# A reordered opening in a one-core retention-and-GELU kernel: identity and single loads first, wider filler matmuls, w_in triggered behind A of batch 0, chunk 1 loaded in one queue

## The chip, the cores and the metric

The kernel runs on one core of a Trainium2 chip. The core has five engines that run their own instruction streams in order: TensorE (PE, with its weight loads shown apart as PEld), VectorE (DVE), ScalarE (ACT), GpSimd (POOL) and SyncE (SP). SP, ACT and POOL also issue DMAs, each into a queue of its own. The metric is the device time of one execution in microseconds (us).

## The reference

A retention recurrence for 4 batches, 8 heads, 768 positions and head size 64, followed by a two-matrix feed-forward block with a tanh GELU:

```python
gamma = 1.0 - 2.0 ** (-5.0 - np.arange(H))
for t in range(S):
    state = gamma[None, :, None, None] * state + np.einsum('bhd,bhe->bhde', k[:, :, t], v[:, :, t])
    y[:, :, t] = scale * np.einsum('bhd,bhde->bhe', q[:, :, t], state)
x = y.transpose(0, 2, 1, 3).reshape(B * S, H * D)          # 3072 x 512
h = x @ w_in                                               # 512 x 2048
g = 0.5 * h * (1.0 + np.tanh(c * (h + 0.044715 * h * h * h)))
out = g @ w_out                                            # 2048 x 512
```

All inputs and the output are float32.

## The kernel before

**Tiling.** The 768 positions are cut into six chunks of 128. For a chunk `c` and a batch `b` the attention part consists of small steps, each a group of PE instructions followed by a copy out of PSUM:

- `prep1`: q and k are scaled by decay columns of the constants `cst` and become f16, v becomes f16. The engine is an argument (VE, AC, PO stand for DVE, ACT, POOL).
- T (`mm_T`, `ev_T`): eight 128x128 transposes of q and k with the identity `iden`, and a copy to `qkT`.
- A (`mm_A`, `ev_A`): eight matmuls give the score tiles `a_ps`; DVE multiplies them by a mask into `a_sb`.
- Y (`mm_yc`, `mm_yi`, `ev_Y`): the part from the state (none in chunk 0) and eight matmuls of v with `a_sb`; the result becomes `xT`.
- S (`mm_s`, `ev_S`): the update of the state `st`.

The feed-forward part then works on `xT` of all four batches (512 columns): `moe1` computes h for one block of 128 of the 2048 features and applies GELU on ACT; `moe1_two` does two blocks for a part of the columns; `moe2` multiplies with `w_out`. Chunks 2 to 5 use a variant with fewer matmuls and more sums on DVE and POOL (`m1_parts`, `m2_parts`); the change does not touch it.

**Order.** The schedule is written by hand: each engine executes its instructions in the order of the program text. In the opening (lines 108 to 117) the loads of chunk 0 go out on SP and ACT. `load1` loads one batch (256 KB), `load2` two batches (512 KB), `load` a whole chunk (1 MB). The weights `w_in` and `w_out` are cast to f16 by DMAs that POOL issues (`load_w_in`, `load_w_out`, four of each); they stand in POOL's queue between its `prep1` steps.

`spin(n)` (line 126) issues `n` f32 matmuls of a zero tile into a PSUM bank whose content nobody reads; they are filler work for PE. In `before` the zero tile is f16 with 512 columns, read as f32 with 256 columns.

**Chunk 0** (lines 667 to 730): T, A and Y of the four batches with fillers between them, then h of features 0 to 3 in three column stages (batches 0 and 1, batch 2, batch 3), S, and `moe1` for features 4 to 15.

**Chunk 1's loads** (lines 732 to 763): q and k of chunk 1 use the same buffers as those of chunk 0. `hold` (line 106) lets POOL write one element of the q buffer after a given tile is there, so that SP's first load must wait for it: once for the third quarter of `w_out`, once for the GELU of feature 10. SP then loads q and k batch by batch. v of chunk 1 is loaded by ACT: batches 0 and 1 in the middle of `moe1` of chunk 0, 2 and 3 behind it. Then `run` interleaves `moe2` of chunk 0 (16 units) with attention steps of chunk 1 after given units. The loads of chunk 2's q and k follow behind all of that on SP.

PSUM has eight banks: two for tag "h", two for "o", four for "att", taken in turn.

Of the kernel before, what the change touches and what calls it, by code (L numbers as in the profile page):

```python
# [9 lines left out]
F16 = mybir.dt.float16  # L10
F32 = mybir.dt.float32
# [5 lines left out]
def kernel(  # L17
# [9 lines left out]
    nc = tc.nc  # L27
    B, H, S, Dh = q.shape
    C = 128
    NCk = S // C  # L30
    NHP = H // 2
# [19 lines left out]
    iden_h = nc.inline_tensor(iden_np, name="rr_ident")  # L51
# [5 lines left out]
    const = ctx.enter_context(tc.tile_pool(name="const", bufs=1))  # L57
    ld = ctx.enter_context(tc.tile_pool(name="ld", bufs=2 * B))
    pre = ctx.enter_context(tc.tile_pool(name="pre", bufs=2 * B))
    att = ctx.enter_context(tc.tile_pool(name="att", bufs=4))  # L60
# [27 lines left out]
    def load1(eng, nm, c, b):  # L88
        eng.dma_start(
            out=ld_tile(nm, c, b),  # L90
            in_=srcs[nm][b, :, c * C:(c + 1) * C, :].rearrange("h p d -> p h d"),
        )

    def load2(eng, nm, c, b):
        eng.dma_start(
            out=raw_of(nm, c)[:, b * H:(b + 2) * H],
            in_=srcs[nm][b:b + 2, :, c * C:(c + 1) * C, :].rearrange("b h p d -> p (b h) d"),
        )

    def load(nm, c, eng=nc.sync):  # L100
        eng.dma_start(
            out=raw_of(nm, c),
            in_=srcs[nm][:, :, c * C:(c + 1) * C, :].rearrange("b h p d -> p (b h) d"),
        )
# [3 lines left out]
        nc.gpsimd.tensor_copy(out=ld_tile(nm, c, b)[0:1, 0, 0:1], in_=until)  # L108

    nc.sync.dma_start(out=cst[:, :OT + 128], in_=cst_h.ap())  # L110
    load2(nc.scalar, "q", 0, 0)
    load2(nc.sync, "k", 0, 0)
    load2(nc.scalar, "q", 0, 2)
    nc.sync.dma_start(out=iden, in_=iden_h.ap())
    load2(nc.sync, "k", 0, 2)
    load2(nc.sync, "v", 0, 0)
    load2(nc.sync, "v", 0, 2)


    zero = const.tile([128, 512], F16, name="zero")  # L120
    nc.vector.memset(zero, 0.0)
    nc.scalar.activation(
        out=misc[:, 0:1], in_=zero[:, 0:1], func=AF.Gelu_apprx_tanh, scale=1.0
# [2 lines left out]
    def spin(n):  # L126
        ps = bank("h", shape=(128, 512), name="spin_ps")
        for _ in range(n):
            nc.tensor.matmul(  # L129
                out=ps[:, 0:256], lhsT=zero.bitcast(F32)[:, 0:128], rhs=zero.bitcast(F32), start=True, stop=True  # L130
            )


# [22 lines left out]
    def prep1(eng, nm, c, b):  # L156
        t = pre.tile(
            [128, H, Dh], F16, tag=f"{nm}16", bufs=B, name=f"{nm}16"
        )
        src = ld_tile(nm, c, b)  # L160
        if (nm == "v") == (c < 2):
            copy_on(eng, t, src)
        else:
            col = OQ if nm == "q" else OK
            eng.tensor_tensor(  # L165
                out=t,
                in0=src,
                in1=cst[:, col:col + H].unsqueeze(2).broadcast_to([128, H, Dh]),
                op=ALU.mult,
            )  # L170
        h16[nm, c, b] = t
# [5 lines left out]
    a_sb = {}  # L177
# [9 lines left out]
    def bank(tag, dt=F32, shape=(128, NHP, 128), name="ps"):  # L187
        turn[tag] += 1
        return bank_at(BANKS[tag][(turn[tag] - 1) % len(BANKS[tag])], dt, shape, name)
# [15 lines left out]
    def ev_T(c, b, eng=nc.vector):  # L205
        copy_on(eng, qkT_of(c, b), pss.pop(("T", c, b)))
# [8 lines left out]
    def mm_A(c, b):  # L215
        t = qkT[c, b]
        ps = [bank("att", name=f"a_ps{j}") for j in range(2)]
        for hp in range(NHP):
            for j in range(2):
                nc.tensor.matmul(  # L220
                    out=ps[j][:, hp],
                    lhsT=t[j * 64:(j + 1) * 64, 1, hp],
                    rhs=t[j * 64:(j + 1) * 64, 0, hp],
                    start=True,
                    stop=True,
                )
        pss["A", c, b] = ps

    def ev_A(c, b):
        ps = pss.pop(("A", c, b))  # L230
        for j in range(2):
            s = att.tile([128, NHP, 128], F16, tag=f"a{j}", bufs=2, name=f"a_sb{j}")
            nc.vector.tensor_tensor(out=s, in0=ps[j], in1=mask[:, j], op=ALU.mult)  # L233
            a_sb[c, b, j] = s

    def mm_yc(c, b, tag):
        y_ps = pss["Y", c, b] = bank(tag, name="y_ps")
        if c == 0:
            return

        for hp in range(NHP):
            for j in range(2):
                sl = slice(j * 64, (j + 1) * 64)
                nc.tensor.matmul(  # L244
                    out=y_ps[sl, hp],
                    lhsT=st[sl, b, hp],
                    rhs=qkT[c, b][sl, 0, hp],
                    start=(hp == 0),
                    stop=False,
                    skip_group_check=True,  # L250
                )

    def mm_yi(c, b):
        y_ps = pss["Y", c, b]
        for hp in range(NHP):
            for j in range(2):
                nc.tensor.matmul(  # L257
                    out=y_ps[j * 64:(j + 1) * 64, hp],
                    lhsT=h16["v", c, b][:, 2 * hp + j],
                    rhs=a_sb[c, b, j][:, hp],  # L260
                    start=(c == 0),
                    stop=True,
                    skip_group_check=True,
                )
# [78 lines left out]
    NO = 4  # L343
    w_out_sb = [const.tile([128, NF // NO, d_model], F16, name=f"w_out{i}") for i in range(NO)]

    def load_w_in(i):
        nc.gpsimd.dma_start(
            out=w_in_sb[i],
            in_=moe_w_in.rearrange("(kc p) n -> p kc n", p=128)[
                :, :, w_in_at[i] * 128:(w_in_at[i] + w_in_n[i]) * 128  # L350
            ],
        )

    def load_w_out(i):
        n = NF // NO
        nc.gpsimd.dma_start(
            out=w_out_sb[i],
            in_=moe_w_out.rearrange("(fc p) n -> p fc n", p=128)[:, i * n:(i + 1) * n],
        )
# [26 lines left out]
        moe1_mm(c, fc, h_ps, 0, B * C)  # L386
        gelu(g_tile(c, fc)[:, fc % 2], h_ps)

    def moe1_two(c, fp, t0, t1):

        h_ps = bank("h", shape=(128, 2, B * C // 2), name="h_ps")
        for r in range(2):
            moe1_mm(c, 2 * fp + r, h_ps[:, r, 0:t1 - t0], t0, t1)
        gelu(g_tile(c, 2 * fp)[:, :, t0:t1], h_ps[:, :, 0:t1 - t0])
# [269 lines left out]
    half = 2 * C  # L664


    def pre_T(b, after=0):
        spin(after)
        mm_T(0, b)
        ev_T(0, b, AC)  # L670

    spin(6)
    for b in (0, 1):
        prep1(VE, "q", 0, b)
        prep1(PO, "k", 0, b)
    load_w_in(0)
    pre_T(0)
    pre_T(1)
    spin(1)
    mm_A(0, 0)  # L680
    ev_A(0, 0)
    mm_A(0, 1)
    prep1(VE, "q", 0, 2)
    ev_A(0, 1)
    prep1(VE, "q", 0, 3)
    for b in (2, 3):
        prep1(PO, "k", 0, b)
    for i in range(1, 4):
        load_w_in(i)
    load_w_out(0)  # L690
    spin(2)
    pre_T(2)
    prep1(AC, "v", 0, 0)
    prep1(AC, "v", 0, 1)
    spin(2)
    mm_A(0, 2)
    ev_A(0, 2)
    mm_yc(0, 0, "o")
    mm_yi(0, 0)
    pre_T(3)  # L700
    mm_yc(0, 1, "o")
    mm_yi(0, 1)
    ev_Y(0, 0, AC)
    ev_Y(0, 1, VE)
    prep1(PO, "v", 0, 2)
    prep1(PO, "v", 0, 3)
    for i in range(1, NO):
        load_w_out(i)
    spin(1)
    mm_A(0, 3)  # L710
    ev_A(0, 3)


    t01 = (0, half)
    moe1_two(0, 0, *t01)
    mm_yc(0, 2, "o")
    mm_yi(0, 2)
    ev_Y(0, 2, AC)
    moe1_two(0, 1, *t01)
    mm_yc(0, 3, "o")  # L720
    mm_yi(0, 3)
    ev_Y(0, 3)
    for t in ((half, half + C), (half + C, 2 * half)):
        for fp in range(2):
            moe1_two(0, fp, *t)
    for bs in ((0, 1), (2, 3)):
        mm_s(0, bs)
        ev_S(0, bs)
# [4 lines left out]
    for fc in range(6, NF):  # L733
        moe1(0, fc)
        if fc % 2 and fc < 14:
            win_sums(VE, (fc - 7) // 2)
        if fc in (8, 10):
            load1(AC, "v", 1, (fc - 8) // 2)
        if fc == 11:
            hold("q", 1, 0, g_tile(0, 10)[0:1, 0, 0:1])  # L740

# [7 lines left out]
    def preps(c, b):  # L749
# [1 line left out]
        prep1(PO, "k", c, b)  # L751
        prep1(AC, "v", c, b)

    load1(SY, "q", 1, 0)
    load1(SY, "k", 1, 0)
    load1(SY, "q", 1, 1)
    load1(SY, "k", 1, 1)
    load1(SY, "q", 1, 2)
    load1(SY, "k", 1, 2)
    load1(SY, "q", 1, 3)  # L760
    load1(SY, "k", 1, 3)
    load1(AC, "v", 1, 2)
    load1(AC, "v", 1, 3)
    u = [units2(0, b, tag="ooho"[b]) for b in range(B)]
    run(
        [u[i % 3][i // 3] for i in range(12)] + u[3],
# [5 lines left out]
            8: [(preps, 1, 0)],  # L772
            10: [(att_T, 1, 0), (preps, 1, 1)],
            11: [(att_AY, 1, (), "att", 1, (0,), None)],
            12: [(att_T, 1, 1), (preps, 1, 2)],
            13: [(att_AY, 1, (0,), "h", 1, (1,), AC)],
            14: [(att_T, 1, 2), (preps, 1, 3), (att_S, 1, 0)],
            15: [(att_AY, 1, (1,), "h", 1, (2,), AC), (att_T, 1, 3), (att_S, 1, 1)],
# [2 lines left out]


    nc.sync.dma_start(out=dec.rearrange("p h t -> p (h t)"), in_=dec_h.ap())
    load("q", 2)
    load("k", 2)

    def cast(nm, c, *bs):
        for b in bs:
# [155 lines left out]
```

## Time and profile before

| What | Value |
|---|---|
| median of 3 runs | 206.59 us (206.44 to 206.8) |
| profiled execution | 206.57 us, span 204.8 us, mean granted PE clock 0.983 |
| DVE, ACT, POOL busy | 129.3, 119.4, 110.4 us |
| constants `cst`: issue, landing | 0.74 us, 2.3 us later |
| identity: issue to landing | 7.0 us |
| w_in, issue to landing (4 DMAs of 512 KB) | 6.7 to 11.4 us, median 8.5 |
| first w_in trigger, first w_out trigger | 8.76 us, 14.73 us |
| first q load of chunk 1 | 33.97 us |
| DMA: moved in the span | 33.73 MB, mean 165 GB/s |

The profiled execution has a span from the first to the last instruction and some 1.8 us around it. The page gives busy time of each engine, the chain of work that ended last (followed back from the last instruction to what released each step), and groups of instructions. The timeline lists instructions in order with start and duration, and what ended the idle time before. The granted clock is the share of full speed that PE's throttle allowed. Line numbers (L129 and the like) are those of the kernel before.

### The profile page before, as it was taken

Reading aid. Unit: us, or ns where it says so; the run is one execution under the profiler, and the core shown is the slowest. Engines: PE = TensorE matmul, PEld = TensorE weight load, DVE = VectorE, ACT = ScalarE, POOL = GpSimd, SP = SyncE. Lnnn points to the kernel's source line nnn. Section 1 sums busy time; section 2 is a strip of 40 time slices with the busy share of each in tenths; the row PEclk is TensorE's granted clock in tenths of the full one; section 3 lists DMA queues with packets and bytes.
Section 4 is the critical chain, followed back from the end, with each engine's and each line's share of the span. In section 5 each row is a group of like instructions: output and inputs, shape, how many; then the busy total and the mean of one; then the engine's idle time right before and its main releaser. Section 6 shows DMA issues by size and latency. Waiting matters only on the chain.

```text
span 204.8 us, 5174 instructions
## 1 busy us (share of the span) xinstructions
PE 194.8 (95%) x2104; PEld 154.1 (75%) x2104; DVE 129.3 (63%) x260; ACT 119.4 (58%) x225; POOL 110.4 (54%) x113
## 2 busy tenths in 40 slices
PE   7398999999999989999999999999999999999993
PEld 6375744445678877788887888888888888888882
DVE  2267399429876789889853888836697723445421
ACT  2036566133478458853978585878555687675411
POOL 0596000124104992826399948399955797599000
PEclk9769999999999999999999999999999999999999
DMA  7999999999899994479959979433100230002204
GB/s 160 284 233 223 207 206 214 287 216 277 256 326 230 275 283 78 103 98 299 274 126 215 255 199 244 103 130 131 26 3 0 90 118 0 5 0 102 106 25 179
DMA packets 60663, 33.73 MB, mean 165 GB/s; under 512 B 40864, under 2 KB 57632, under 8 KB 60640
## 3 DMA queue, kind: packets, MB, share of 16 engines
q1 hardware_dynamic: 44640, 23.18, 45.6%
q0 software_dynamic: 4304, 4.46, 12.7%
q10 hardware_dynamic: 11696, 5.77, 10.7%
q8 instruction: 16, 0.26, 0.5%
q14 instruction: 7, 0.06, 0.1%
HBM read 27.63 MB, written 6.29 MB: 166 GB/s over the span
## 4 chain that ended last, share of the span: by engine, by line
PE 86%; DMA 5%; DVE 3%; ACT 3%; issue 1%; SPq 0%; DVEq 0%
PE o_ps L510 28%; PE h_ps L625 23%; PE h_ps L366 14%; PE o_ps L400 7%; DMA iden<-rr_ident 3%; PE y_ps L257 3%; PE a_ps L220 3%; PE y_ps L244 3%; PE qkT_ps L195 3%; PE spin_ps L129 1%; PE s_ps L281 1%; DVE xT L273 1%; DMA qkT<-k 1%; ACT qkT L152 1%; ACT g L382 1%
## 5 line engine op out<-in xcount | busy, mean ns | idle before, releaser
L437 POOL TENSOR_TENSOR s_g<-g 128x512 f16<-128x512 f16 x34 | 38.7, 1152 | 11.8 <-ACT g L382 11.8
L382 ACT ACTIVATE g<-h_ps 128x512 f16<-128x512 f32 (+1 forms) x50 | 29.0, 581 | 19.9 <-PE h_ps L366 14.2
L233 DVE TENSOR_TENSOR a_sb<-a_ps,mask 128x512 f16<-128x512 f32 x48 | 30.2, 684 | 9.5 <-PE a_ps L220 7.9
L510 PE MATMUL o_ps<-t_w,s_g 128*128 128x256 f16 x240 | 34.2, 273 | 0.0
L510 PEld LDWEIGHTS <-s_g 128*128 128x128 f16 x320 | 31.3, 98 | 3.6
L366 PE MATMUL h_ps<-xT,w_in 128*128 128x256 f16 (+2 forms) x224 | 30.4, 288 | 0.1
L625 PE MATMUL h_ps<-t_x,s_w 128*128 128x256 f16 x192 | 28.9, 273 | 0.3 <-DVE h_p L437 0.3
L625 PEld LDWEIGHTS <-s_w 128*128 128x128 f16 x256 | 24.5, 98 | 4.5 <-issue 1.2
L366 PEld LDWEIGHTS <-w_in 128*128 128x128 f16 x224 | 19.7, 98 | 7.9 <-issue 0.2
L510 PEld LDWEIGHTS <-g 128*128 128x128 f16 x240 | 23.4, 98 | 2.8
L510 PE MATMUL o_ps<-w_out,g 128*128 128x256 f16 x160 | 22.9, 273 | 0.0
L437 POOL TENSOR_TENSOR s_g<-s_g,g 128x512 f16<-128x512 f16 x17 | 19.6, 1156 | 4.6 <-PE o_ps L510 3.4
L165 POOL TENSOR_TENSOR v<-v,cst 128x512 f16<-128x512 f32 x16 | 16.2, 1037 | 10.7 <-DMA v<-in_v_dram 10.7
L642 ACT COPY h_u<-h_ps 128x512 f32<-128x512 f32 x16 | 9.4, 586 | 21.3 <-PE h_ps L625 21.2
L437 DVE TENSOR_TENSOR h_q<-h_ps,h_q 128x512 f32<-128x512 f32 x16 | 11.1, 692 | 16.3 <-PE h_ps L625 10.5
L625 PEld LDWEIGHTS <-w_in 128*128 128x128 f16 x192 | 18.3, 98 | 3.4 <-issue 0.7
L437 DVE TENSOR_TENSOR h_p<-h_ps,h_p 128x512 f32<-128x512 f32 x16 | 11.0, 690 | 13.9 <-ACT h_p L642 9.6
L437 POOL TENSOR_TENSOR s_g<-g,s_g 128x512 f16<-128x512 f16 x17 | 19.5, 1155 | 0.5
L625 PE MATMUL h_ps<-xT,w_in 128*128 128x256 f16 x128 | 19.2, 272 | 0.3 <-ACT g L382 0.3
L165 POOL TENSOR_TENSOR k<-k,cst 128x512 f16<-128x512 f32 x8 | 8.4, 1054 | 18.1 <-DMA k<-in_k_dram 15.5
L437 DVE TENSOR_TENSOR o_sb<-o_ps,o_sb 128x512 f32<-128x512 f32 (+1 forms) x18 | 10.8, 597 | 7.6 <-PE o_ps L510 7.3
L400 PE MATMUL o_ps<-w_out,g 128*128 128x512 f16 x64 | 14.8, 379 | 0.0
(70 smaller groups left out, 302.4 us busy)
## 6 DMA issues: line engine op xcount, KB each, us to landing
out_dram<-o_sb SPq DMA_DIRECT2D x8, 512.0 KB, 2.7
w_in<-in_moe_w_in_dram POOLq DMA_DIRECT2D x4, 512.0 KB, 8.5
w_out<-in_moe_w_out_dram POOLq DMA_DIRECT2D x4, 512.0 KB, 13.7
q<-in_q_dram ACTq DMA_DIRECT2D x2, 512.0 KB, 6.0
k<-in_k_dram SPq DMA_DIRECT2D x2, 512.0 KB, 5.6
v<-in_v_dram SPq DMA_DIRECT2D x2, 512.0 KB, 8.0
v<-in_v_dram ACTq DMA_DIRECT2D x4, 256.0 KB, 6.5
q<-in_q_dram SPq DMA_DIRECT2D x4, 256.0 KB, 5.2
```

Source lines behind the costliest of these rows:

```text
L165: eng.tensor_tensor(out=t, in0=src, in1=cst[:, col:col + H].unsqueeze(2).broadcast_to([128, H, Dh]), op=ALU.mult,)
L195: nc.tensor.transpose(out=ps[:, i, hp], in_=pair(h16[nm, c, b], hp), identity=iden)
L220: nc.tensor.matmul(out=ps[j][:, hp], lhsT=t[j * 64:(j + 1) * 64, 1, hp], rhs=t[j * 64:(j + 1) * 64, 0, hp], start=True, stop=True,)
L233: nc.vector.tensor_tensor(out=s, in0=ps[j], in1=mask[:, j], op=ALU.mult)
L244: nc.tensor.matmul(out=y_ps[sl, hp], lhsT=st[sl, b, hp], rhs=qkT[c, b][sl, 0, hp], start=(hp == 0), stop=False, skip_group_check=True,)
L366: nc.tensor.matmul(out=out, lhsT=w_in_sb[wi][:, kc, wr * 128:(wr + 1) * 128], rhs=xT[c][:, kc, t0:t1], start=(kc == 0), stop=(kc == NHP - ...
L382: nc.scalar.activation(out=out, in_=in_, func=AF.Gelu_apprx_tanh, scale=1.0)
L400: nc.tensor.matmul(out=ps[:, n0:n1], lhsT=g_sb[c, fc // 8][:, fc % 8, b * C:(b + 1) * C], rhs=w_out_sb[fc // (NF // NO)][:, fc % (NF // NO ...
L437: eng.tensor_tensor(out=out, in0=in0, in1=in1, op=op)
L510: nc.tensor.matmul(out=po, lhsT=lhs(c, lk, fp, a), rhs=rhs(rk, fp), start=(new and fp == 0 and (last or a == 0)), stop=(fp == NP - 1), ski ...
L625: nc.tensor.matmul(out=p[:, f], lhsT=w, rhs=x, start=(new and f == 0 and kk == 0), stop=(kk == 1), skip_group_check=True,)
L642: nc.scalar.copy(out=snap[nm], in_=p)
```

## The change

The change touches the opening and the loads of chunks 1 and 2.

- Loads: q and k of batches 0 and 1 are loaded singly, alternating between ACT and SP; the identity goes out on ACT second, not on SP third; k of batches 2 and 3 on SP and q of batches 2 and 3 on ACT follow.
- The zero tile becomes f32 with 512 columns, and a filler matmul takes all 512.
- `a_sb` gets four buffers for each half, where it had two.
- The opening's order: T(0), A(0), T(1), A(1), T(2), T(3), A(2), Y(0), A(3), Y(1), Y(2), then h, with fillers of 8, 2, 2, 3, 1 and 1. q of batch 2 is scaled ahead of A(1)'s masks. A one-element copy on POOL that reads `a_sb` of batch 0 stands ahead of the first `load_w_in`, and with it behind A(0). The last `w_in` and all of `w_out` follow behind the casts of v for batches 2 and 3.
- h of batch 2's columns uses the "att" banks.
- Chunk 1: q, k and v all go on SP, v in pairs of batches behind k of batches 1 and 2; the whole q of chunk 2 follows on SP at once, and k of chunk 2 is issued behind unit 12.

```diff
     nc.sync.dma_start(out=cst[:, :OT + 128], in_=cst_h.ap())
-    load2(nc.scalar, "q", 0, 0)
-    load2(nc.sync, "k", 0, 0)
+    load1(nc.scalar, "q", 0, 0)
+    load1(nc.sync, "k", 0, 0)
+    nc.scalar.dma_start(out=iden, in_=iden_h.ap())
+    load1(nc.sync, "q", 0, 1)
+    load1(nc.scalar, "k", 0, 1)
+    load2(nc.sync, "k", 0, 2)
     load2(nc.scalar, "q", 0, 2)
-    nc.sync.dma_start(out=iden, in_=iden_h.ap())
-    load2(nc.sync, "k", 0, 2)
     load2(nc.sync, "v", 0, 0)
     load2(nc.sync, "v", 0, 2)
...
-    zero = const.tile([128, 512], F16, name="zero")
+    zero = const.tile([128, 512], F32, name="zero")
...
             nc.tensor.matmul(
-                out=ps[:, 0:256], lhsT=zero.bitcast(F32)[:, 0:128], rhs=zero.bitcast(F32), start=True, stop=True
+                out=ps, lhsT=zero[:, 0:128], rhs=zero, start=True, stop=True
             )
...
-            s = att.tile([128, NHP, 128], F16, tag=f"a{j}", bufs=2, name=f"a_sb{j}")
+            s = att.tile([128, NHP, 128], F16, tag=f"a{j}", bufs=4, name=f"a_sb{j}")
...
-    def pre_T(b, after=0):
-        spin(after)
+    def pre_T(b, eng=AC):
         mm_T(0, b)
-        ev_T(0, b, AC)
-
-    spin(6)
+        ev_T(0, b, eng)
+
+    def pre_A(b):
+        mm_A(0, b)
+        ev_A(0, b)
+
+    def pre_Y(b, eng=AC):
+        mm_yc(0, b, "o")
+        mm_yi(0, b)
+        ev_Y(0, b, eng)
+
+    spin(8)
     for b in (0, 1):
         prep1(VE, "q", 0, b)
         prep1(PO, "k", 0, b)
+    pre_T(0)
+    spin(2)
+    pre_A(0)
+    pre_T(1)
+    nc.gpsimd.tensor_copy(out=misc[0:1, 2:3], in_=a_sb[0, 0, 0][0:1, 0, 0:1])
     load_w_in(0)
-    pre_T(0)
-    pre_T(1)
-    spin(1)
-    mm_A(0, 0)
-    ev_A(0, 0)
-    mm_A(0, 1)
+    spin(2)
     prep1(VE, "q", 0, 2)
-    ev_A(0, 1)
+    pre_A(1)
     prep1(VE, "q", 0, 3)
     for b in (2, 3):
         prep1(PO, "k", 0, b)
-    for i in range(1, 4):
+    for i in (1, 2):
         load_w_in(i)
-    load_w_out(0)
-    spin(2)
+    spin(3)
     pre_T(2)
+    spin(1)
+    pre_T(3, VE)
+    pre_A(2)
     prep1(AC, "v", 0, 0)
     prep1(AC, "v", 0, 1)
-    spin(2)
-    mm_A(0, 2)
-    ev_A(0, 2)
-    mm_yc(0, 0, "o")
-    mm_yi(0, 0)
-    pre_T(3)
-    mm_yc(0, 1, "o")
-    mm_yi(0, 1)
-    ev_Y(0, 0, AC)
-    ev_Y(0, 1, VE)
+    pre_Y(0)
+    pre_A(3)
+    pre_Y(1)
     prep1(PO, "v", 0, 2)
     prep1(PO, "v", 0, 3)
-    for i in range(1, NO):
+    load_w_in(3)
+    for i in range(NO):
         load_w_out(i)
     spin(1)
-    mm_A(0, 3)
-    ev_A(0, 3)
+    pre_Y(2)
...
     moe1_two(0, 0, *t01)
-    mm_yc(0, 2, "o")
-    mm_yi(0, 2)
-    ev_Y(0, 2, AC)
+    pre_Y(3, VE)
     moe1_two(0, 1, *t01)
-    mm_yc(0, 3, "o")
-    mm_yi(0, 3)
-    ev_Y(0, 3)
-    for t in ((half, half + C), (half + C, 2 * half)):
+    for t, tag in (((half, half + C), "att"), ((half + C, 2 * half), "h")):
         for fp in range(2):
-            moe1_two(0, fp, *t)
+            moe1_two(0, fp, *t, tag)
...
-        if fc in (8, 10):
-            load1(AC, "v", 1, (fc - 8) // 2)
...
-    load1(SY, "q", 1, 0)
-    load1(SY, "k", 1, 0)
...
-    load1(AC, "v", 1, 2)
-    load1(AC, "v", 1, 3)
+    for b in range(B):
+        load1(SY, "q", 1, b)
+        load1(SY, "k", 1, b)
+        if b in (1, 2):
+            load2(SY, "v", 1, 2 * b - 2)
+    load("q", 2)
...
-            12: [(att_T, 1, 1), (preps, 1, 2)],
+            12: [(att_T, 1, 1), (preps, 1, 2), (load, "k", 2)],
...
     nc.sync.dma_start(out=dec.rearrange("p h t -> p (h t)"), in_=dec_h.ap())
-    load("q", 2)
-    load("k", 2)
```

More of the change, by code (lines that the diff above doesn't have):

```diff
@@ L387, in moe1, with moe1_two @@
         gelu(g_tile(c, fc)[:, fc % 2], h_ps)
-    def moe1_two(c, fp, t0, t1):
-        h_ps = bank("h", shape=(128, 2, B * C // 2), name="h_ps")
+    def moe1_two(c, fp, t0, t1, tag="h"):
+        h_ps = bank(tag, shape=(128, 2, B * C // 2), name="h_ps")
         for r in range(2):
@@ L752, in preps @@
         prep1(AC, "v", c, b)
-    load1(SY, "q", 1, 0)
-    load1(SY, "k", 1, 0)
[L756 to L761, printed above, removed]
-    load1(AC, "v", 1, 2)
-    load1(AC, "v", 1, 3)
+    for b in range(B):
[4 more added lines that the diff above has]
+    load("q", 2)
     u = [units2(0, b, tag="ooho"[b]) for b in range(B)]
```

## The prediction

> **What bounds the kernel now.** I first read the page's busy shares and its chain that ended last.
>
> ```profile
> PE 194.8 (95%) x2104; PEld 154.1 (75%) x2104; DVE 129.3 (63%) x260; ACT 119.4 (58%) x225; POOL 110.4 (54%) x113
> PE 86%; DMA 5%; DVE 3%; ACT 3%; issue 1%; SPq 0%; DVEq 0%
> ```
>
> TensorE (PE) is busy in 194.8 of 204.8 us, and the chain is PE work for 86% of the span. Whatever moves the point at which the dense feed-forward work begins therefore moves the end by as much. That point is found in the timeline of the opening (start in us, duration in us; the bracket tells what ended the idle time before).
>
> ```profile
> 1.19 4.23 PE L129 MATMUL spin_ps<-zero 128*128 128x256 f32 x12 [1.19 <-DVE zero L121]
> 1.71 3.03 SPq L114 DMA_DIRECT2D iden<-rr_ident  x1
> 6.78 2.04 POOL L165 TENSOR_TENSOR k<-k,cst 128x512 f16<-128x512 f32 x2 [6.33 <-DMA k<-in_k_dram]
> 8.76 0.59 PE L195 MATMUL qkT_ps<-iden,q 128*128 128x128 f16 x4 [3.33 <-DMA iden<-rr_ident]
> 18.45 0.59 ACT L152 CAST xT<-y_ps 128x512 f16<-128x512 f32 x1
> 19.09 1.03 PE L366 MATMUL h_ps<-xT,w_in 128*128 128x256 f16 x8
> ```
>
> Six filler matmuls (12 records, two to a matmul) end at 5.42, PE waits 3.33 us for the identity, and the first h matmul starts at 19.09, when batch 1's xT is out of PSUM (18.45 + 0.59). Afterwards PE hardly stops: the stretch table (length, then busy us of PE, PEld, DVE, ACT, POOL, granted clock, DMA share, GB/s) shows this and the clock.
>
> ```profile
> 5.42:8.76 3.34, 0.01 (x2) 0.10 (x1) 1.24 (x2) 0.00 (x0) 1.99 (x3) 0.80 1.28 288
> 8.76:14.41 5.65, 5.65 (x40) 4.25 (x40) 2.25 (x4) 1.93 (x2) 4.86 (x7) 0.51 1.21 240
> 14.41:19.09 4.68, 4.16 (x56) 2.77 (x53) 3.38 (x7) 3.55 (x5) 2.92 (x5) 1.00 1.25 235
> 24.42:34.96 10.54, 10.54 (x55) 4.82 (x50) 10.34 (x29) 6.57 (x11) 0.44 (x2) 1.00 1.23 206
> 34.96:53.90 18.94, 18.94 (x169) 9.86 (x168) 11.72 (x24) 6.28 (x11) 4.91 (x5) 1.00 1.07 262
> ```
>
> So the opening loses 3.3 us idle and works at half clock from 8.76 until about 14.3. The last view I need is filler matmuls one by one (rows from narrow windows of PE's timeline).
>
> ```profile
> 1.78 1.06 PE L129 MATMUL spin_ps<-zero 128*128 128x256 f32 x2
> 2.21 1.06 PE L129 MATMUL spin_ps<-zero 128*128 128x256 f32 x2
> 2.63 1.06 PE L129 MATMUL spin_ps<-zero 128*128 128x256 f32 x2
> 15.02 0.59 PE L129 MATMUL spin_ps<-zero 128*128 128x256 f32 x2
> 15.24 0.59 PE L129 MATMUL spin_ps<-zero 128*128 128x256 f32 x2
> ```
>
> A record starts 0.425 us after the last one early on, and 0.215 us at full clock; a filler matmul of 256 columns is two records, 0.85 us slow and 0.43 us fast. The early ones are slow although the clock column says 1.00 there: it has no event before 4.02 us, where the pitch changes. The clock rises at 4.02, falls at 7.43 and rises at 14.26, multiples of 3.41 us apart.
>
> **The change, step by step.** Its own time is 206.57 us (span 204.8, 1.8 around it), 0.02 below the median of the runs, 206.59.
>
> *Fillers.* The built order of PE's instructions has 17 fillers (8, 2, 2, 3, 1, 1) where 12 stood (6, 1, 2, 2, 1), and each is 512 columns wide, not 256. No row shows a 512-wide f32 matmul. Bounds: the cost goes with the instruction (0.43 us fast) or with the columns (0.85 fast, 1.70 slow). I take columns: f16 rows on this page take 219 ns at 128 columns (the identity's rows), 273 at 256 and 379 at 512, that is, 54 and 106 more, which doubles with the columns.
>
> *First use of PE.* Memset of zero doubles, 0.27 to 0.54 us, so fillers start at 1.46. With the clock rising at 4.02 as now, 2.56 us slow do 2.56/1.70 = 1.5 of the eight; 6.5 x 0.852 = 5.54 us remain: they end at S = 9.56.
>
> *Loads and identity.* The identity goes second on ACT's queue, batches 0 and 1 go singly. At the 288 GB/s of the row above, from 2.1 us on, cst, q(0), k(0) and the identity (0.63 MB) are in by about 4.5 us; k(0) is scaled by about 5.8 (1.02 on POOL). A late identity as now (8.71) is still ahead of S. So what this gains, up to 3 us, is covered by the fillers: transposes T(0) start at 9.56, not 8.76. I cost the splitting at nothing; if the cover went, one more load's issue is 0.37 to 0.51 us.
>
> The Trainium skill speaks against splitting (DMA: Bandwidth & Descriptors, Rules for kernel authors): at least 1 MiB for each DMA, because of a fixed cost of some 2 us. By that rule two more loads, taken in series, would add an estimated 4 us to the 5.8, and T(0) would start at about 9.8. The rows say otherwise: 512 KB loads ran at 288 GB/s in the opening, and 256 KB ones, from 35 to 40 us, at 283.
>
> *From S to the first h.* All at full clock, since nothing idles: 4 T of 0.45, 4 A and 3 Y of 0.34 (rows of the chain) = 4.18; nine fillers = 7.67; 0.1 for A(3) behind T(3)'s copy on DVE (0.69); five switches into fillers at some 0.05 (the record at 17.77 took 0.48, that at 14.75 took 0.43) = 0.3. Sum 12.2, so h starts at 21.8. The copies lie under it: qkT(0) is out at S + 1.5 (ACT 1.01), fillers last to S + 2.2; xT(1) is out at S + 11.4; q(2) is scaled on DVE by S + 4.6, ahead of A(1)'s masks, used at S + 7.6. Batch 2's Y is now ahead of h, so the point to compare is 19.09 + 0.34 = 19.43: a loss of 2.4 us.
>
> *w_in behind A(0).* POOL's new one-element copy waits for a_sb at S + 3.2 = 12.8; behind it in POOL's queue stand w_in 0, k(2), k(3), w_in 1 and 2, v(2), v(3), w_in 3 and w_out. By 13 us q, k, v (3.15 MB at 288 GB/s) are all in, so w_in 0 meets no other traffic. Issue to landing now takes 6.7 to 11.4 us, the long ones behind other weights; 13.0 + 6.7 = 19.7, ahead of 21.8. k(2) is ready by S + 5.4, w_in 1 is triggered by 17 and wanted at 27. If 11.4 held for the first, h would be 2.6 us later. Eight weights of 512 KB at 206 GB/s are 20.4 us: w_out 2 lands at about 33.5, as now.
>
> *Chunk 1 in one queue.* The first q load waits for w_out 2 and for gelu 10 (now over at 31.3, then 33.7), so starts near 34 as now. All ten loads then stand on SP, v with them, ahead of the whole q of chunk 2 and three stores. SP's pace, 218 GB/s from 40 to 45 us, gives 3.1 MB in 14.4 us, plus 2.5 for w_out 3: the last k at about 50.5, where now it is
>
> ```profile
> 48.15 1.04 POOL L165 TENSOR_TENSOR k<-k,cst 128x512 f16<-128x512 f32 x1 [0.95 <-DMA k<-in_k_dram]
> 53.03 0.40 PE L195 MATMUL qkT_ps<-iden,q 128*128 128x128 f16 x4
> ```
>
> and PE wants it at 53.03 + 2.4: four us of cover, three after scaling. v(0) and v(1) are in by about 44; ACT, which they would block, has its first o copy at 43.63 + 2.4. Nothing; without cover up to 2 us. ACT's v issues (0.37 each, 2.49 blocked) hid behind gelus and earn nothing. More a_sb buffers and the third pair of h banks remove waits that PE doesn't show: 0 to 0.1.
>
> Sum: 206.57 + 2.4 = 209.0.
>
> **Rivals.**
> A, the forecast: 209.0. Its own range, 208.1 to 209.7: the rise of the clock up to 1 us earlier or later is worth half of that shift, and the switches are 0 to 0.5, the wait for A(3) 0 to 0.2.
> B, the clock rises 3.41 us later, at 7.43: fillers fill only 75% of the stretch 0.61 to 4.02 (now 83%). S becomes 1.46 + 5.97 slow + 4.5 x 0.852 = 11.3; time 210.7. The row at half clock from 8.76 to 14.41 speaks for it, PE being busy all that time before the clock came back.
> C, chunk 1's single queue makes PE or ACT wait 1 to 2 us: 210 to 211. Against it: the cover above.
> D, other side: a wide filler costs no more than a narrow one. The eight end at 1.46 + 2.56 + 5.0 x 0.43 = 6.2, T(0) runs then, and w_in 0 (triggered by about 9, 6.7 to land) lets h start at about 16: 203.2. With 15.5 full-clock fillers on the path, it is faster below 0.852 - 2.4/15.5 = 0.70 us for one. For it: PE idles 3.3 us now. Against: the pitch by columns.
> E, the gain of the early identity and the fillers cancel: 206.2 to 207.0, at 0.70 us for a filler.
>
> The Trainium skill (TensorE: Matmul & The Clock Gate, The HAM clock gate) has windows of some 3.4 us that run free of the kernel's start, so the rise can fall anywhere in one; the rises here, at 4.02 and 14.26, are three such windows apart. By it alone a rise at about 5 us would give an estimated 209.4; nothing above uses this.
>
> **How the numbers follow.** A 0.62, B 0.18, C 0.08, D 0.08, E 0.04. Forecast 209.0. The range 208.1 to 210.8 holds A and B and most of C; D, E and the edges are some 0.17. Over 0.2% (0.4 us, about what a measurement tells from no change): slower 0.62 + 0.18 + 0.08 = 0.88, same 0.04, faster 0.08.
>
> **What would show it.** Filler records of 0.85 us pitch, then 0.43; no wait for the identity; T(0) at 9.6; clock 1.00 throughout from 4.0; w_in waits nowhere; h at 21.8; then a constant shift to the end, and no wait of PE between 35 and 55 us. It is wrong if T(0) starts before 8.7, if h starts before 19.4, or if PE stalls for w_in or chunk 1.

## The result and the profile after

| | before | changed |
|---|---|---|
| median, on one chip | 206.69 us (206.44 to 212.39, 4 runs) | 215.91 us (215.17 to 217.47, 4 runs) |
| profiled execution | 206.57 us, span 204.8 | 217.47 us, span 215.7 |

The changed kernel is slower: ratio 1.046, 95% interval 1.038 to 1.054. The direction was forecast; of the loss of 9.3 us (215.91 against 206.59) the forecast had 2.4. The time of the kernel before varies from one execution to the next (205.9 to 216.1 us on the chips used below); ratios are taken among undisturbed executions, and the profiles of `one_queue_alone`, `before_shared`, the repeat of `one_small_load`, `q3_off_the_rotation`, `small_load_narrow` and `identity_early` are of disturbed ones.

The page's busy shares and the chain's shares by engine, of the changed kernel:

```profile
PE 202.9 (94%) x2114; PEld 154.8 (72%) x2114; DVE 130.6 (61%) x260; ACT 119.4 (55%) x225; POOL 111.9 (52%) x114
PE 85%; DMA 6%; DVE 4%; ACT 2%; issue 1%; ACTq 0%; DVEq 0%
```

The page shows little: PE is busy for 8.1 us more, the chain one more point of DMA. The opening's timeline (start, duration, engine) is the first place to look.

```profile
1.22 0.60 ACTq L113 DMA_DIRECT2D iden<-rr_ident  x1
1.45 8.73 PE L131 MATMUL spin_ps<-zero 128*128 128x512 f32 x16 [1.45 <-DVE zero L123]
...
3.32 0.34 PEld L131 LDWEIGHTS spin_ps<-zero 128*128 128x128 f32 x1 [0.52 <-issue]
4.18 0.34 PEld L131 LDWEIGHTS spin_ps<-zero 128*128 128x128 f32 x1 [0.52 <-issue]
...
8.74 0.19 PEld L131 LDWEIGHTS spin_ps<-zero 128*128 128x128 f32 x1 [0.24 <-issue]
9.16 0.19 PEld L131 LDWEIGHTS spin_ps<-zero 128*128 128x128 f32 x1 [0.24 <-issue]
13.64 0.93 POOL L349 DMA_DIRECT2D w_in<-in_moe_w_in_dram  x1
22.83 1.05 PE L368 MATMUL h_ps<-xT,w_in 128*128 128x256 f16 x8
```

Sixteen filler records run 0.86 us apart early and 0.42 late, two to a matmul; they end at 10.18, and the first transposes follow at once, with no wait for the identity. The first h is at 22.83 against the compare point 19.43. The table of stretches (length, busy us of PE, PEld, DVE, ACT, POOL, granted clock, DMA share, GB/s), over the changed kernel's own stages, shows where PE stops:

```profile
1.45:10.19 8.74, 8.74 (x19) 3.87 (x20) 2.56 (x10) 1.49 (x2) 2.31 (x2) 1.00 1.15 261
...
38.08:57.02 18.94, 18.94 (x169) 9.86 (x168) 10.95 (x23) 6.21 (x11) 5.08 (x5) 1.00 0.99 243
57.02:66.00 8.98, 8.98 (x115) 7.02 (x116) 7.20 (x21) 5.43 (x11) 0.00 (x0) 1.00 1.02 300
66.00:70.00 4.00, 0.95 (x11) 0.70 (x9) 0.64 (x4) 0.00 (x0) 0.00 (x0) 0.94 1.56 122
70.00:75.00 5.00, 1.70 (x10) 1.29 (x11) 0.69 (x1) 2.50 (x6) 3.60 (x4) 0.50 0.63 93
```

PE is busy throughout the fillers and from 38.08 to 66. The chain has the `moe1` stage of features 4 to 15 in one row (start, length, instructions), first that of the kernel before, then that of the changed one:

```profile
24.50 10.46 PE h_ps L366 x48
...
27.61 10.47 PE h_ps L368 x48
```

The stretch after that stage takes PE 18.94 us in both: 3.1 us lost in the opening, constant to 58 us. Then PE, ACT and POOL all stand, and the clock drops to half. The timeline there, engine by engine:

```profile
58.23 0.83 ACTq L101 DMA_DIRECT2D v<-in_v_dram  x1
...
71.39 4.03 POOL L167 TENSOR_TENSOR v<-v,cst 128x512 f16<-128x512 f32 x4 [14.64 <-DMA v<-in_v_dram]
71.64 0.13 ACT L101 MOVE_SHAPE q<-in_q_dram  x1 [6.38 <-DMA v<-in_v_dram]
72.62 0.62 ACT L154 CAST k<-k 128x512 f16<-128x512 f32 x1 [0.85 <-POOL v L167]
...
73.30 0.61 PE L197 MATMUL qkT_ps<-iden,k 128*128 128x128 f16 x4 [6.35 <-ACT k L154]
```

Read upwards: PE stood 6.35 us for ACT's cast of k of chunk 2; that cast stood in ACT's queue behind the issue of another load, q of chunk 3; and that issue stood 6.38 us for the load of v of chunk 2, of which it uses nothing. The data that PE wanted was there: each transfer counts its semaphore up sixteen times as its parts land, and in the trace the last count of k of chunk 2 came at 65.94, before PE stopped at 66.95. In the kernel before the same issue waits for nothing; v is in before POOL's work on it starts at 64.29:

```profile
61.73 0.72 ACTq L101 DMA_DIRECT2D q<-in_q_dram  x1
64.29 2.04 POOL L165 TENSOR_TENSOR v<-v,cst 128x512 f16<-128x512 f32 x2 [10.66 <-DMA v<-in_v_dram]
```

Why a load of q waits for a load of v stands in the compiled programs, in the list of what each instruction waits for (the transfers that SP and ACT issue take eight completion semaphores, DMAHW0 to DMAHW7, in turn, and a transfer waits until the earlier one with its number is done):

```text
                    v of chunk 2 signals   q of chunk 3 signals, and waits for
kernel before       DMAHW2                 DMAHW5   (5, 7, 4, 3)
changed kernel      DMAHW5                 DMAHW5   (7, 5, 2)
```

The change took loads off ACT's queue, paired others, and put k of chunk 2 behind unit 12; with that the turn moved, and the two loads fell eight places apart (v is the 22nd transfer in the turn and q the 30th; in the kernel before they are the 27th and the 30th). The sum for the profiled execution: 3.1 (opening) + 6.35 (the stop) + some 1.55 (3.1 us of work, 73.30 to 76.39, at half clock) = 11.0; its span is 10.9 longer.

### The profile page after: what moved, and what is told of

It reads as the page before. It is cut to its first block, busy times and chain, and to the rows that moved or that the text cites. A ratio compares the mean times of both kernels' runs of the same rounds, so it can differ in the third digit from the quotient of the medians.

```text
span 215.7 us, 5174 instructions
## 1 busy us (share of the span) xinstructions
PE 202.9 (94%) x2114; PEld 154.8 (72%) x2114; DVE 130.6 (61%) x260; ACT 119.4 (55%) x225; POOL 111.9 (52%) x114
## 3 DMA queue, kind: packets, MB, share of 16 engines
q0 software_dynamic: 4304, 4.46, 12.7%
## 4 chain that ended last, share of the span: by engine, by line
PE 85%; DMA 6%; DVE 4%; ACT 2%; issue 1%; ACTq 0%; DVEq 0%
PE o_ps L512 27%; PE h_ps L627 22%; PE h_ps L368 10%; PE spin_ps L131 8%; PE o_ps L402 7%; DMA v<-in_v_dram 6%; PE a_ps L222 3%; PE y_ps L259 3%; PE qkT_ps L197 2%; PE y_ps L246 2%; DVE xT L275 1%; PE s_ps L283 1%; ACT g L384 1%; DVE t_x L439 1%; DVE st L300 0%
## 5 line engine op out<-in xcount | busy, mean ns | idle before, releaser
L384 ACT ACTIVATE g<-h_ps 128x512 f16<-128x512 f32 (+1 forms) x50 | 28.9, 580 | 19.8 <-PE h_ps L368 14.4
L368 PE MATMUL h_ps<-xT,w_in 128*128 128x256 f16 (+2 forms) x224 | 31.0, 293 | 0.0
L368 PEld LDWEIGHTS <-w_in 128*128 128x128 f16 x224 | 20.2, 100 | 8.0
L627 PEld LDWEIGHTS <-w_in 128*128 128x128 f16 x192 | 18.3, 98 | 3.4 <-issue 0.7
L627 PE MATMUL h_ps<-xT,w_in 128*128 128x256 f16 x128 | 19.2, 272 | 0.3 <-ACT g L384 0.3
L167 POOL TENSOR_TENSOR k<-k,cst 128x512 f16<-128x512 f32 x8 | 9.3, 1170 | 18.8 <-DMA k<-in_k_dram 11.7
L131 PE MATMUL spin_ps<-zero 128*128 128x512 f32 x34 | 17.6, 657 | 1.5 <-DVE zero L123 1.5
L156 DVE COPY qkT<-qkT_ps 128x1024 f16<-128x1024 f16 x7 | 4.8, 690 | 18.4 <-PE qkT_ps L197 18.4
```

The costliest lines, as they stand in the source:

```text
L131: nc.tensor.matmul(out=ps, lhsT=zero[:, 0:128], rhs=zero, start=True, stop=True)
L167: eng.tensor_tensor(out=t, in0=src, in1=cst[:, col:col + H].unsqueeze(2).broadcast_to([128, H, Dh]), op=ALU.mult,)
L368: nc.tensor.matmul(out=out, lhsT=w_in_sb[wi][:, kc, wr * 128:(wr + 1) * 128], rhs=xT[c][:, kc, t0:t1], start=(kc == 0), stop=(kc == NHP - ...
L384: nc.scalar.activation(out=out, in_=in_, func=AF.Gelu_apprx_tanh, scale=1.0)
L627: nc.tensor.matmul(out=p[:, f], lhsT=w, rhs=x, start=(new and f == 0 and kk == 0), stop=(kk == 1), skip_group_check=True,)
```

## The experiments

Sizes are us. Several runs share a chip and its runs of the kernel before, which are given where they matter.

**1. The two halves of the change, apart.** `opening_alone` is the changed kernel with the loads of chunks 1 and 2 as before; `one_queue_alone` is the kernel before with the changed loads of chunks 1 and 2:

```diff
-    load1(SY, "q", 1, 0)
...
-    load1(AC, "v", 1, 3)
+    for b in range(B):
+        load1(SY, "q", 1, b)
+        load1(SY, "k", 1, b)
+        if b in (1, 2):
+            load2(SY, "v", 1, 2 * b - 2)
+    load("q", 2)
...
+            12: [(att_T, 1, 1), (preps, 1, 2), (load, "k", 2)],
```

> The changed kernel with the chunk 1 and chunk 2 loads of before (v of chunk 1 on ACT, q and k of chunk 2 at the end). Both theories: the opening's loss alone, 3.1 us, time 209 to 210.5, with no stop of PE between 55 and 80 us. If the opening is what delays the loads, 213 or more.

> The kernel before with the changed loads of chunks 1 and 2 alone. Here too the q load of chunk 3 shares its semaphore with the v load of chunk 2. Theory (shared semaphore): ACT stops for v of chunk 2 as in the changed kernel, 4 to 7 us, and PE behind it: 211 to 215. Rival (the late opening and the one queue act together): 206.5 to 208, because k and v of chunk 2 are on the way earlier.

`opening_alone` gave 210.31 to 210.82 (median 210.44; ratio 1.014, 1.010 to 1.019): no stop of PE at 67, and `moe1` starts at 28.26, 3.8 behind the kernel before. `one_queue_alone` gave 213.28 to 217.06. Its timeline has the same stop, shorter, since v took 9.4 here, not 13.0 (PE stood 2.57 for the cast of k behind it):

```profile
69.90 0.02 ACT L101 MOVE_SHAPE q<-in_q_dram  x1 [2.40 <-DMA v<-in_v_dram]
```

The profiled execution, at 216.68, holds another stop, of 4.4 in the opening, that has nothing to do with the edit (experiment 4). So the opening is worth some 3 to 4 (2.9 by the ratio, 3.8 by the start of `moe1`), and the stop at 67 to 72 belongs to the loads.

**2. The shared semaphore, made and unmade.** `before_shared` adds five loads of 2 KB to the kernel before, only so that q of chunk 3 comes eight transfers after v of chunk 2. `one_small_load` adds one such load to the changed kernel, so that it comes nine after. `changed_again` is the changed kernel.

```diff
+            2: [(small, 5), (cast, "q", 2, 0, 1)],
...
+    nc.sync.dma_start(out=misc[:, 8:12], in_=cst_h.ap()[:, 0:4])
```

> The kernel before with five loads of 16 bytes per partition on SP behind the second pair of chunk 1's feed-forward blocks, so that the q load of chunk 3 takes the semaphore of the v load of chunk 2, which lands at about 64.2 where q is issued at 61.7. Theory (shared semaphore): ACT stops 2 to 2.5 us there and PE nearly as long: 208 to 209.2. Rival (loads too late by themselves): 206.4 to 207, the five loads being nothing.

> The changed kernel with one more load of 16 bytes per partition on SP behind the dec load. DMAs on SP and ACT take their completion semaphores from eight in rotation, and in the changed kernel the q load of chunk 3 on ACT has the one of the v load of chunk 2, eight places before it; with one more DMA between them it gets the next. Theory (shared semaphore): ACT no longer waits for v of chunk 2, PE's stop of 6.4 us and the 1.5 us at half clock behind it go, v still lands late; time 209 to 210, that is, 206.6 and the opening's 3.1. Rival (the loads themselves are too late for PE, because chunk 1 and 2 go through one queue): 214 to 217, as the changed kernel.

> The changed kernel once more, beside the others of this set. Theory (shared semaphore): the stop of ACT ends when v of chunk 2 has landed, so it is 2.4 us where that load takes 9.4 us and 6.4 us where it takes 13; time 212 to 217.5. If the stop is the same 6.4 us whatever the load takes, the theory is incomplete.

> The kernel of one_small_load once more, for more runs: the changed kernel with one 2 KB load more, so that the load of q of chunk 3 no longer shares a completion semaphore with the load of v of chunk 2. Theory, the shared semaphore is the only loss behind 58 us: ACT waits for no load between 55 and 75, and the median is 209.5 to 211, as opening_alone's 210.44. Rival, the single queue of chunk 1 costs something of its own in some executions: the median is 213 or more, and where the profile is one of those it shows PE waiting for a load or a cast of chunk 1 or 2 between 35 and 75.

In `before_shared` the stop appeared where it was put, as its timeline shows. The totals, 211.38 to 219.85, missed the 208 to 209.2 of the theory; the profiled execution, at 219.85, also holds the opening's other stop, 7.0 there:

```profile
73.54 0.02 ACT L101 MOVE_SHAPE q<-in_q_dram  x1 [2.40 <-DMA v<-in_v_dram]
```

`changed_again` gave 215.92 to 218.23 (ratio 1.046, 1.038 to 1.054), ACT standing 4.94 with v 11.6 after its issue. There k of chunk 2 itself was in at 68.89 only, so of PE's 4.90 an estimated 2.6 would have stood without the semaphore too (0.75 from k's landing to PE, as in `v_half_filled_5`). `one_small_load` was profiled at 210.16, with no wait of ACT for v and none of PE above 0.73, as expected; its row of ACT:

```profile
65.43 0.13 ACT L101 MOVE_SHAPE q<-in_q_dram  x1
```

But its other runs were 213.54, 214.33 and 217.63, and the repeat gave a median of 215.63 (211.12 to 215.77), which is the rival's total, though not with the wait that the rival named. The repeat's profile tells most of it; SP's and PE's timeline:

```profile
70.59 1.19 SPq L212 DMA_TRANSPOSE qkT<-q  x1
...
80.68 0.40 PE L222 MATMUL a_ps<-qkT 64*128 64x128 f16 x8 [3.14 <-DMA qkT<-k]
```

The eighth transfer after v is now SP's second transpose of q. By SP's waits it stood 4.0 for v (2.3 in the execution at 210.16, where v landed at 68.1), the transposes of k behind it were late, and PE stood 3.14 (0.73). With `moe1` 0.5 later and the clock at half from 81.56 to 84.98 (up to 1.7) this makes up to 4.6 of the 5.6 between the two profiles. The wait had been moved from ACT to SP, not removed; how much of it reaches PE depends on when v lands.

**3. All early transfers off v's semaphore.** `q3_off_the_rotation` issues `dec` and q of chunk 3 from GpSimd, whose transfers use other semaphores; `partner_last` issues there two small transfers instead, so that v shares with the last transpose of k alone; `k2_early` keeps the sharing and loads k of chunk 2 and `dec` early, out of v's way.

```diff
-    nc.sync.dma_start(out=dec.rearrange("p h t -> p (h t)"), in_=dec_h.ap())
+    nc.gpsimd.dma_start(out=dec.rearrange("p h t -> p (h t)"), in_=dec_h.ap())
...
-            5: [(load, "q", 3, AC), (cast, "k", 2, 0), (cast, "v", 2, 0, 1, 2, 3)],
+            5: [(load, "q", 3, PO), (cast, "k", 2, 0), (cast, "v", 2, 0, 1, 2, 3)],
...
-        eng = nc.sync if b < B - 1 else nc.gpsimd
+        eng = nc.sync if b < B - 2 else nc.gpsimd
...
+    load("k", 2)
```

> The changed kernel with two loads, dec and q of chunk 3, issued from GpSimd's queue, which doesn't take part in the rotation of eight completion semaphores of SP's and ACT's transfers. By the program's wait lists, what waits for v of chunk 2 is then not ACT's load of q (changed kernel) nor the second transpose of q (the two runs with one small load more, where SP issued that transpose when v had landed, at 68.1 and near 70.6, and PE then waited 0.7 and 3.1 for the transpose of k), but the last transpose of k, which is issued near 70 anyway. Theory, who shares v's semaphore is the whole loss behind 58 us: ACT and SP stop for v at most 1 to 2 and PE at most 1 between 55 and 80; every run lies within 1.5 of the others, median 209.5 to 211.3, as opening_alone's 210.44. Rival, chunk 1 in one queue costs by the lateness of its data or by v's own slowness: PE waits 2 or more for chunk 2's v, k or q whoever shares the semaphore; median 213 or more.

> The changed kernel with two small transfers (dec, and the store of batch 2's rows of chunk 0, 256 KB each) issued by GpSimd, where the run before this one had moved the 1 MB load of q of chunk 3 and had k of chunk 2 land 17 us after its issue, at 76.2, beside it. By the wait lists v of chunk 2 now shares its semaphore with the last transpose of chunk 2's k alone, and ACT's load of q of chunk 3 waits for none that is late. Theory, the shared semaphore is the loss behind 58 us: q of chunk 3 is issued near 65.6, ACT stops for no load of 1 MB between 58 and 72, PE stands less than 1 for the last transpose; median 209.5 to 212. Rival, the single queue brings k and v of chunk 2 late by itself: PE stands 2 or more between 60 and 80 for k or v whatever shares; median 213 or more.

> The changed kernel with dec and k of chunk 2 loaded directly behind q of chunk 2, as the kernel before has them, where the change put them behind unit 12 and all units; v of chunk 2 and q of chunk 3 still share semaphore 5. In the kernels with k's load 2.5 or more ahead of v's, v took 9.0 to 9.7 (before, opening_alone, one_queue_alone, before_shared), with k 0.2 to 1.5 ahead 9.5 to 13.0. Theory, v is slow where k's load runs beside it: v takes 9.0 to 9.7, ACT stands 2 to 3.2 for it, PE 2 to 3, total 211.5 to 213.5. Rival, v's slowness is not k's: v takes 11 or more and ACT stands 4.5 or more, total 215 to 217.5.

`q3_off_the_rotation` gave 217.44 (216.24 to 221.44): worse. ACT no longer waits for v, but 1 MB of q now runs beside k and v, k lands 17.4 after its issue, ACT's cast of k stands for it, and PE 9.66 for the cast:

```profile
58.81 0.71 SPq L101 DMA_DIRECT2D k<-in_k_dram  x1
76.28 0.62 ACT L154 CAST k<-k 128x512 f16<-128x512 f32 x1 [10.67 <-DMA k<-in_k_dram]
```

So the time of the data is close behind the semaphore. `partner_last` gave 212.42 (210.83 to 213.9; ratio 1.023, 1.013 to 1.034), just above the theory's 212 and below the rival's 213; PE's wait of 1.50 also lies between the two. No engine waits for v but POOL, which needs it; what is left is 1.5:

```profile
66.28 2.33 ACTq L101 DMA_DIRECT2D q<-in_q_dram  x1
...
69.38 0.40 PE L197 MATMUL qkT_ps<-iden,k 128*128 128x128 f16 x4 [1.50 <-ACT k L154]
```

The issue itself took 2.33 there, where it takes 0.72 in the kernel before. With `moe1` at 28.54 in this run (4.0 lost in the opening), the loads cost 2.0 of the rest of the span. `k2_early` missed its theory: v's work on POOL starts 10.8 after the issue of v, not 9.7, ACT stood 4.0 (its row names a store, for which by the compiled program it does not wait; v was in 0.4 before ACT went on), and the kernel gave 216.46 (216.19 to 216.98). k was in at 62.88 there, so PE's 3.96 is the semaphore's alone. k's load beside it is not what makes v slow, or not alone.

**4. The opening's fillers, and w_in beside v.** `opening_narrow` is `opening_alone` with fillers of 256 columns; `small_load_narrow` is `one_small_load` with them; `identity_early` is the kernel before with the identity second on ACT's queue.

```diff
-    zero = const.tile([128, 512], F32, name="zero")
+    zero = const.tile([128, 256], F32, name="zero")
...
+    nc.scalar.dma_start(out=iden, in_=iden_h.ap())
     load2(nc.scalar, "q", 0, 2)
-    nc.sync.dma_start(out=iden, in_=iden_h.ap())
```

> The changed opening with before's loads of chunks 1 and 2, and fillers of 256 columns (the same 17). Theory (the fillers are the opening's whole loss): T(0) starts near 6.2 instead of 10.2, h starts between 15.5 and 18, time 202.5 to 205.5. Rival (the opening's new order, or w_in behind A(0), costs too): 206 or more, with PE waiting for w_in or for copies ahead of h.

> The whole change with the small load that separates the semaphores, and fillers of 256 columns. If chunk 1's single queue has enough cover even with an earlier opening: as the opening with narrow fillers, 202.5 to 205.5. If the single queue is late once PE is 3 to 5 us earlier: 1 to 3 us more than that.

> The kernel before with one edit: the identity is issued second on ACT's queue instead of third on SP's. T(0) starts when k(0) is scaled, at 7.8 to 8.0 instead of 8.76, so of the 3.3 us that PE waits less than 1 us is to be had: 205.6 to 206.2. If the identity were what bounds the opening, 203.5.

`opening_narrow`: 208.67 (205.89 to 213.82), ratio 1.001 (0.994 to 1.007). `moe1` starts at 25.39, 2.9 earlier than in `opening_alone`, so the fillers' width is most of the opening's loss. But the gain that was expected beyond that (202.5 to 205.5) did not come; the opening's timeline of `opening_narrow`:

```profile
18.04 1.17 POOL L156 CAST v<-v 128x512 f16<-128x512 f32 x2 [3.28 <-DMA v<-in_v_dram]
18.71 0.41 PE L259 MATMUL y_ps<-a_sb,v 128*64 128x128 f16 x8 [2.02 <-POOL v L156]
```

The first w_in is triggered at 10.27, before v of chunk 0 is in, and v of batches 2 and 3 is there at 18.0. In `small_load_narrow` (w_in at 9.33; 210.82 to 217.48, above what either of its theories had) it was 25.3, in `identity_early` (w_in at 8.96; 209.34 to 213.32, none of the 205.6 to 206.2 that were expected) 24.0, in `one_queue_alone` (9.11) 22.8. In `opening_alone` w_in starts at 14.30, and nothing waits for v.

**5. w_in behind v.** `v_first` and `v_half_first` are `opening_narrow` with the first w_in triggered when the last, or the first, half of v has landed; `before_v_first` is the kernel before with the first of these; `v_half_filled` and `v_half_filled_5` put ten and five fillers in front of h.

```diff
-    load_w_in(0)
...
+    nc.gpsimd.tensor_copy(out=misc[0:1, 2:3], in_=ld_tile("v", 0, 2)[0:1, 0, 0:1])
+    load_w_in(0)
```

> opening_narrow (the changed opening with 256-column fillers, the loads of chunks 1 and 2 as before) with the trigger of the first w_in moved behind the landing of chunk 0's v (a one-element GpSimd copy that reads the raw v of batches 2 and 3). Theory, v's last packets crawl when the weights' packets start before they are through: v lands at about 12 to 13 us as in the changed kernel, the first w_in is triggered at about 13 and lands at about 17.5, so the h stage starts at 17.5 to 18.5 against 19.43 in the kernel before; total 204.0 to 205.8, all runs within 1 us of each other, as opening_alone's were. Rival, v's lateness has nothing to do with the weights: PE still waits 2 us or more for v's preparation on GpSimd in the profile, and the runs spread over several us, as opening_narrow's (205.89 to 213.82).

> The kernel before with one edit: the trigger of the first w_in waits for the raw v of batches 2 and 3 of chunk 0. Theory: the runs lie within 1 us of each other; the first w_in lands some us later than before, which costs the h stage up to 1 us: 206.2 to 207.8. Rival, v's lateness has nothing to do with the weights: the runs spread as those of the kernel before did on some chips, 206.1 to 216.

> v_first with the first w_in triggered when the first half of v (batches 0 and 1) has landed, not the second. In v_first's profile the second half landed at 14.4, the trigger was at 14.56, the first w_in landed 5.61 later, at 20.16, and PE stood 3.6 for it with its work of chunk 0 done at 16.55; the DMA engines moved almost nothing from 14 to 16 (18, 0 and 58 GB/s). Theory, only a start beside v's packets hurts, and the weights' packets begin 1.5 after the trigger: trigger at 12.6 to 12.8 behind GpSimd's preparations of k, landing at 18.2 to 18.5, h stage then, in place of 19.1 in the kernel before; PE stands 1.8 and keeps the full clock; total 204.8 to 206.0 with a spread below 1.5. Rival, the tail of v still meets the weights: PE waits for v's preparation on GpSimd, v lands after 16, 206.5 to 212 with a spread of several us.

> v_half_first with ten 256-column fillers in front of the first h stage. In v_half_first PE stood 2.8 for the first w_in, which landed at 19.2, and the granted clock fell: its eight first h products took 1.89 where they take 0.98 at full clock, and the kernel gave 209.23. Theory, the standing itself costs nothing against the kernel before (h at 19.2 against 19.1), the lost clock does: ten fillers of 0.22 to 0.27 keep PE busy from 16.4 to 19, the h stage starts at 19.2 to 19.6 at full clock; 206.2 to 207.6, spread below 1.5. Rival, the clock is not held by fillers or another stop follows: 208.5 or more.

> v_half_filled with five fillers instead of ten in front of the first h stage. There ten took 4.51 minus the y_ps step, 0.22 to 0.23 for each of two passes, kept the clock at full (mean 1.00) and ended at 21.64, some 2.3 after the first w_in could be used. Five end near 19.4: h at 19.4 to 19.8 at full clock, against 19.1 before; 206.0 to 207.2 where nothing is disturbed. Rival, w_in lands later than in v_half_first: PE waits for it and the total stays above 208.

PE waited for v in none of their profiles. The opening of `v_first`, its timeline and then one stretch:

```profile
14.44 0.17 POOL L696 COPY misc<-v 1x1 f32<-1x1 f32 x1 [1.81 <-DMA v<-in_v_dram]
14.56 0.93 POOL L349 DMA_DIRECT2D w_in<-in_moe_w_in_dram  x1
20.21 1.89 PE L368 MATMUL h_ps<-xT,w_in 128*128 128x256 f16 x8 [3.63 <-DMA w_in<-in_moe_w_in_dram]
```

```profile
15.00:16.00 1.00, 1.00 (x14) 0.55 (x10) 1.00 (x3) 0.91 (x2) 1.00 (x2) 1.00 0.00 0
```

The runs lie closer together (`v_first` 209.77 to 211.03, `v_half_first` 208.46 to 210.2), but 3 to 6 above the totals expected: the DMA engines move almost nothing from 14 to 16 us, w_in lands 5.6 after its trigger, and PE's wait costs the clock too (1.89 for eight products that take 1.05 in the changed kernel). With the clock held by fillers, `v_half_filled` gave 208.47 (207.97 to 214.51), where 206.2 to 207.6 was expected, ten fillers being some 2 too long (h at 21.5, where `v_half_first` had it at 19.2). Five gave 212.3 (210.51 to 213.6) on a chip where the kernel before ran at 207.01 to 215.57, and its profile has PE standing 2.22 for k of chunk 2 and 1.73 for its transpose, without any semaphore shared early. `before_v_first` gave 210.71, 210.94, 210.97 and 216.93, above its 206.2 to 207.8: `moe1` began 1.25 later and PE stood 2.61 for k of chunk 2, which landed 14.9 after its issue. None of these beats the kernel before (ratios from 1.008, 1.005 to 1.012, for `v_half_filled`, to 1.022).

## Why the prediction was right in sign and wrong in size

- *What bounds the kernel*: right. 3.1 us in the opening moved everything up to 58 us by 3.1.
- *Fillers by columns*: right, 1.71 slow and 0.855 fast for one, against 1.70 and 0.852. Rival D, on which the faster side stood, needed under 0.70.
- *First use of PE*: fillers from 1.45 (1.46 forecast) to 10.18, not 9.56. The clock rose at 4.70, not 4.02, which is 0.34 by the forecast's own rule of half the shift. That rule holds: rises at 4.62, 4.70, 5.43 and 6.01 (`changed_again`, changed, `one_small_load`, `opening_alone`) have `moe1` at 27.57, 27.61, 27.97 and 28.26, that is 0.69 for 1.39, and the latest rise with this opening, 6.57 in `partner_last`, has it at 28.54. Rival B's rise at 7.43 came in none of the eight executions profiled with this opening.
- *From S to h*: 12.7 against 12.2; five groups of fillers took 8.27 (1.77, 1.77, 2.77, 0.91, 1.05) against 7.67 plus 0.3 for the switches. So h lost 3.4, not 2.4; the h stage, shorter by some 0.3, gave that back. The term is 0.7 too small in the profiled execution, and 1.4 too small by the start of `moe1` in `opening_alone`. The rise (0.34) and the filler groups (0.3) make 0.6 of the 1.0 by which h was later than forecast; the rest is not assigned.
- *Identity, w_in*: right. No wait of PE for either; w_in 0 was triggered at 13.64 (12.8), when v of chunk 0 was almost in (14.68). But the last of the weights came later than forecast, w_out 2 at 37.0 and not at 33.5.
- *Chunk 1 in one queue*: the step that failed. "Nothing; without cover up to 2 us" was worked out from when chunk 1's data land. There was no wait of PE from 35 to 55, but with less cover than was forecast. The changed kernel's rows:

```profile
37.12 0.41 POOL L108 CAST q<-w_out 1x1 f32<-1x1 f16 x1 [13.64 <-DVE t_w L439]
37.88 0.37 SPq L89 DMA_DIRECT2D q<-in_q_dram  x1
54.28 1.04 POOL L167 TENSOR_TENSOR k<-k,cst 128x512 f16<-128x512 f32 x1 [3.96 <-PE s_ps L283]
56.38 0.39 PE L197 MATMUL qkT_ps<-iden,k 128*128 128x128 f16 x4
```

The first load waited for w_out 2, whose last part landed at 37.01 (the bracket names another of POOL's waits, a sum on DVE), and went out at 37.88, not near 34; the last k was in at 54.15, not 50.5. Scaled at 55.32 and used at 56.38, it had 1.1 us of cover, not three, and 0.7 of that came from PE itself being later than forecast (56.15 for the transposes of that batch, 55.4 forecast). That this part held was luck.

The "constant shift to the end" did not hold. The step moved and removed transfers, counted each one's place in SP's queue, and did not ask what moves with their number: on which earlier transfer each later one waits. Experiments 2 and 3 show it: the stop appears in the kernel before when only the count is changed, it moves to SP when the count is changed by one, and it goes when v shares with a late transfer. Its size, 2.3 to 6.4 for PE, goes with v's landing, 9.4 to 13.0 after its issue. Rival C had the right edit, another mechanism, and too low a price.

- What stays open: why v takes 13.0 in one execution and 9.4 in another (k's load beside it was tried and is not enough). The traces say only what is late: fourteen of v's sixteen parts were in by 66.92 in the changed kernel, 8.7 after the issue, and the last two at 69.27 and 71.25; in the kernel before all sixteen were in 9.0 after. Also open is how much the single queue costs with no semaphore shared early. `partner_last` has 2.0 in one profile, of which PE's 1.50 follows a slow issue on ACT.

## What to carry to other kernels

In programs compiled as these are, adding, removing or pairing a transfer on one queue changes which later transfers wait for which earlier ones, on every queue that shares the completion semaphores: list these pairs before and after, and look for a long load whose partner is issued while it runs. A load issued by an engine that also computes stops the computing when its semaphore is taken. And filler work whose end comes after the thing it covers is plain work: count it at full price.

## What was not expected of the hardware

- Late tails: v of chunk 0 is requested before w_in, but where w_in started at 8.84 to 10.27 (`before_shared`, `identity_early`, `one_queue_alone`, `small_load_narrow`, `opening_narrow`) v was in at 18.0 to 26.2, and in `v_first`, where w_in waits for v, v was in at 14.4. The kernel before itself triggers w_in at 8.76, with v in at 17.26; how late it is differs between executions. Again it is the last part that is late: in `small_load_narrow` fifteen of the sixteen were in by 18.41 and the last at 25.25. In the traces v's packets there are of 256 B (some 18 ns each) and the weights' of 1,024 B (some 98 ns). The Trainium skill (DMA: Bandwidth & Descriptors, Queues, rings and completion order) has each DMA engine take its queues in turn, a packet at a time, a packet there being several descriptors; if the packets of the trace are served in the same way, a load of small packets yields to one of larger packets, and the late tails agree with it, but no run here isolates it.
- A load of 1 MB of chunk 2's k took 13.5 to 17.4 us in some executions (`v_half_filled_5`, `before_v_first`, `q3_off_the_rotation`), where it took 9.2 in the changed kernel.
- The fillers' rise of the clock, at 4.02 in the kernel before, came between 4.62 and 6.57 in the eight executions profiled with the changed opening's wide fillers, though PE's fillers started within 0.3 us of the same time. The Trainium skill (TensorE: Matmul & The Clock Gate, The HAM clock gate) has windows that run free of the kernel's start, and these rises agree with that.
